# Windowed attention and a top-1 mixture of experts: a smaller ring of keys, and second weights of expert 0 split at the end of attention

## The chip, the cores and the metric

One core of a Trainium2 chip runs the whole program as one launch. The metric is the time of the launch on the device in microseconds (us); lower is better. TensorE is called PE here, VectorE DVE, ScalarE ACT, GpSimd POOL, and SyncE SP; SP issues most of the DMAs and POOL the indirect ones.

## What is computed

Attention over 8 batches, 8 heads, 576 positions and 64 features per head: four heads look back over a window of 32, four over 128 in steps of 4. Its output, 4608 rows of 512, goes into a top-1 mixture of 8 experts with 1024 hidden units.

```python
scores = q @ k.T / sqrt(64), masked by the window of the head
x = softmax(scores) @ v, rows of all heads side by side      # [4608, 512]
logits = x @ w_gate
e = argmax(logits); gate = softmax(logits)[e]
out = gate * (relu(x @ w1[e]) @ w2[e])                        # row by row
```

All of it is in float32. The products of the experts are made from a high and a low part of each operand (`wu` holds both parts of a weight unit, `raw` the unit as loaded): ACT casts `raw` into the high part, and DVE subtracts it from `raw` for the low part.

## The kernel before

**Attention.** 36 tiles of 128 query rows (4 pairs of batches, 9 tiles each) run through a software pipeline, `step(n)`: scores of tile n, transposes of the probabilities of n-1 (`st_trans`, `st_ptcopy`), the product with v and the normalised rows of n-2 (`st_av`, `st_x`), transposes of n-3 and logits of n-4. SP loads q and k of a tile as one transfer (`load_qk`, 576 KB, 128 rows of 4608 bytes) and v as another (`load_v`, 520 KB). The tile `qkr` has 6 slots and `vr` 6; `step(n)` issues `load_qk(n + 5)` and `load_v(n + 3)`. Each tile's keys are loaded whole, that is 128 of its own and the 32 before them.

**Routing.** After the ninth tile of a pair, `route(m)` finds each row's expert and place: logits transposed (`tl`), maximum (`mx`), one-hot (`oh`), running counts (`cs`), and three small matmuls on PE (`rk`, in `rank`), from which DVE selects (`sel`) and works out block and place. For pairs 0 to 2, POOL scatters the row numbers into tables in memory (`tab`). Pair 3 does it on PE instead: for each of its nine tiles DVE makes two matrices, `s` (L554) and `b` (L562) in `mark`, and PE adds their product into `tb` (L573, `enter`). `read_table` reads the three tables back over SP, `add_tables` adds them on POOL (L674, L675), and three DVE instructions make `rows_all` (L437) of `tb` and the tables. From `rows_all` POOL gathers the rows of each expert's blocks (`xg`, L746). While `hold` is on, work set aside for PE waits; it is set for pair 2.

**Experts.** For rows that were routed early, expert 0's first layer (`layer1`: matmuls `s` and `hps`, L900, then `x` and `h` on DVE, L912) runs at the end of attention; its second layer is `layer2` (`yps`, L931). Its second weights are units 4 to 7 of 512 KB; units 4 to 6 are loaded early into `raw`, unit 7 after attention. The rest of the rows of expert 0 comes in blocks `r0`, `r1` (`rest0`): gather, transposes `tpx` (L970), two layers; then experts 1 to 7. From `with tc.manual_schedule` after attention (L1437) the order of all engines is the order of the code.

**What sets the order.** Through step 34 (`MEND`) the order of PE, DVE and ACT is that of the code; behind it, up to L1437, a scheduler orders each engine's instructions by priority. SP's and POOL's order is the scheduler's in all of attention. Each engine executes strictly in the order given. Tiles come from pools; a pool that lies over memory of closed pools first waits for the work on it.

```python
    for key, bufs in (("h", 9), ("w1", 4), ("w2", 4), ("x1", 1), ("d", 1), ("y", 2)):
        pools[key] = ctx.enter_context(tc.tile_pool(name="p" + key, bufs=bufs))
...
    for f in range(4, 8):
        st_.layer1([f])
        raw = early.pop(f) if f in early else st_.load(f)
        st_.units.append(split_unit(1, raw))
```

## Time and profile before

| what | value |
|---|---|
| median of 3 runs | 606.92 us (606.56 to 608.8) |
| the profiled execution, its own time | 606.45 us |
| its span in the trace | 604.7 us |
| PE busy | 585.5 us (97% of the span) |
| DVE, ACT, POOL busy | 363.6, 315.3, 188.3 us |
| mean granted clock of TensorE | 0.991 |
| moved by DMA | 152.52 MB, mean 252 GB/s |

The span is the traced stretch of one execution; the 1.75 us between it and that execution's own time lie around it. In the order of time, attention runs to some 165 us, the routing of the last pair and the first expert's early rows from there to some 195 us, then the experts. A busy time is the sum of an engine's instructions. An idle time counts only where the engine is the one that the end waits for.

### The profile page before, as it was taken

Reading aid. Unit: us, or ns where it says so; the run is one execution under the profiler, and the core shown is the slowest. Engines: PE = TensorE matmul, PEld = TensorE weight load, DVE = VectorE, ACT = ScalarE, POOL = GpSimd, SP = SyncE. Lnnn points to the kernel's source line nnn. Section 1 sums busy time; section 2 is a strip of 40 time slices with the busy share of each in tenths; the row PEclk is TensorE's granted clock in tenths of the full one; section 3 lists DMA queues with packets and bytes.
Section 4 is the critical chain, followed back from the end, with each engine's and each line's share of the span. In section 5 each row is a group of like instructions: output and inputs, shape, how many; then the busy total and the mean of one; then the engine's idle time right before and its main releaser. Section 6 shows DMA issues by size and latency. Waiting matters only on the chain. (4 is left out here: it accounts for less than half of the span.)

```text
span 604.7 us, 13500 instructions
## 1 busy us (share of the span) xinstructions
PE 585.5 (97%) x5175; PEld 478.7 (79%) x5175; DVE 363.6 (60%) x786; ACT 315.3 (52%) x612; POOL 188.3 (31%) x234
## 2 busy tenths in 40 slices
PE   7999999999989999999999999999999999999995
PEld 6877778777777888888888888888888888888784
DVE  3877888887758457636564566457547646663200
ACT  2568776766723555534555466456536554662210
POOL 0346676486573225140033022202300330031011
PEclk8999999999999999999999999999999999999998
DMA  8999999995325538985778679778868786779411
GB/s 333 409 372 412 411 406 408 398 344 162 86 56 176 186 130 278 244 272 171 206 256 298 176 250 296 239 201 288 265 223 241 253 306 173 236 260 405 177 42 46
DMA packets 67522, 152.52 MB, mean 252 GB/s; under 512 B 15040, under 2 KB 31360, under 8 KB 67424
## 3 DMA queue, kind: packets, MB, share of 16 engines
q1 hardware_dynamic: 55744, 121.50, 59.5%
q0 software_dynamic: 11712, 30.14, 14.1%
q8 instruction: 41, 0.67, 0.5%
q14 instruction: 25, 0.20, 0.1%
HBM read 124.02 MB, written 28.60 MB: 252 GB/s over the span
## 5 line engine op out<-in xcount | busy, mean ns | idle before, releaser
L931 PE MATMUL yps<-wu,h 128*128 128x512 f32 x696 | 164.4, 392 | 0.0
L721 DVE TENSOR_TENSOR wu<-raw,wu 128x512 fp32r<-128x512 f32 x200 | 128.3, 687 | 55.7 <-ACT wu L720 49.9
L900 PE MATMUL hps<-x,wu 128*128 128x512 f32 (+1 forms) x720 | 161.6, 383 | 0.2 <-DVE h L912 0.2
L900 PEld LDWEIGHTS hps<-x,wu 128*128 128x128 f32 x720 | 132.3, 188 | 27.4 <-DVE h L912 0.8
L931 PEld LDWEIGHTS yps<-wu,h 128*128 128x128 f32 x696 | 129.4, 188 | 27.4 <-issue 0.6
L720 ACT CAST wu<-raw 128x512 fp32r<-128x512 f32 x200 | 112.9, 618 | 12.2 <-DMA raw<-in_w_dram 11.9
L796 POOL DMA_INDIRECT out_dram<-y,rows_all x30 | 30.4, 1012 | 197.8 <-ACT y L795 85.2
L912 DVE SCALAR_TENSOR_TENSOR h<-hps,h 128x512 fp32r<-128x512 f32 (+1 forms) x60 | 40.2, 671 | 52.4 <-ACT h L911 51.1
L911 ACT ACTIVATE h<-hps 128x512 fp32r<-128x512 f32 (+1 forms) x60 | 35.0, 583 | 62.5 <-PE hps L900 49.6
L323 ACT COPY pts<-pt 96x512 f32<-96x512 f32 x72 | 41.9, 582 | 46.9 <-PE pt L318 40.3
L746 POOL DMA_INDIRECT xg<-x_d,rows_all x30 | 32.0, 1065 | 95.0 <-DVE x L791 35.3
L297 DVE TENSOR_REDUCE nm<-s 128x4 f32<-128x384 f32 x72 | 39.7, 552 | 25.7 <-PE s L286 20.7
L318 PE MATMUL pt<-ident,p 128*96 128x128 f32 x288 | 47.5, 289 | 4.9 <-ACT pts L323 4.2
L795 ACT ACTIVATE y<-yps,gate 128x512 f32<-128x512 f32 x30 | 20.7, 688 | 45.5 <-PE yps L931 37.1
L333 PEld LDWEIGHTS o<-vr,pts 96*64 96x64 f32 x1152 | 37.9, 139 | 7.2 <-issue 6.1
L333 PE MATMUL o<-vr,pts 96*64 96x65 f32 x1152 | 43.1, 226 | 0.4 <-issue 0.4
L302 DVE TENSOR_TENSOR d<-s,nm 128x384 f32<-128x384 f32 x72 | 40.1, 557 | 4.6
L312 ACT ACTIVATE p<-d 128x384 f32<-128x384 f32 x72 | 37.6, 524 | 6.5 <-DVE d L302 6.5
L1037 PE MATMUL ypd<-wu,hd 128*128 128x512 f32 x168 | 40.7, 391 | 0.0
L365 POOL DMA_DIRECT2D x_d<-xs x36 | 20.6, 571 | 63.0 <-DVE xs L353 25.7
L1005 PE MATMUL hpd<-wu,xd 128*128 128x512 f32 x168 | 39.9, 391 | 0.0
L318 PEld LDWEIGHTS pt<-ident,p 128*96 128x96 f32 x288 | 28.9, 128 | 13.0 <-ACT pts L323 5.3
(161 smaller groups left out, 627.0 us busy)
## 6 DMA issues: line engine op xcount, KB each, us to landing
raw<-in_w_dram SPq DMA_DIRECT2D x104, 512.0 KB
qkr<-in_qk_dram SPq DMA_DIRECT2D x36, 576.0 KB
vr<-in_v_dram SPq DMA_DIRECT2D x36, 520.0 KB
rows<-xg SPq DMA_DIRECT2D x29, 264.0 KB
xg<-rows SPq DMA_DIRECT2D x116, 64.0 KB
wu<-in_w_dram SPq DMA_DIRECT2D x12, 512.0 KB
x_d<-xs POOLq DMA_DIRECT2D x44, 128.0 KB
wz<-in_w_dram SPq DMA_DIRECT2D x4, 512.0 KB
```

Source lines behind the costliest of these rows:

```text
L297: nc.vector.tensor_reduce(st["nm", n][:, g], st["s", n][g], axis=AX.X, op=ALU.max)
L302: nc.vector.tensor_tensor(st["d", n][:, g], st["s", n][g], st["nm", n][:, g].broadcast_to([P, HP, KB]), op=ALU.subtract,)
L318: nc.tensor.transpose(pt[:KB, h], st["p", n][:, g, h], ident)
L323: nc.scalar.copy(st["pts", n][:, g], st.pop(("pt", n))[:KB])
L333: nc.tensor.matmul(st["o", n][QB * j : QB * (j + 1), g, h], lhsT=pts[:, g, h, QB * j : QB * (j + 1)], rhs=vr[:KB, n % NRV, a : a + DH + 1] ...
L720: nc.scalar.copy(u[:, 0, sl], raw[:, sl])
L721: nc.vector.tensor_tensor(u[:, 1, sl], raw[:, sl], u[:, 0, sl].bitcast(F32), op=ALU.subtract)
L900: nc.tensor.matmul(hps[:, : self.ns], lhsT=u[:, wpart, fs], rhs=self.x[:, xpart, c, : self.ns], start=(k == 0), stop=(k == 11),)
L912: nc.vector.scalar_tensor_tensor(h[:, 1, :n], hps[:, :n], 0.0, h[:, 0, :n].bitcast(F32), op0=ALU.max, op1=ALU.subtract,)
L931: nc.tensor.matmul(yps, lhsT=self.h[f][:, hpart, ts], rhs=u[:, wpart, fs], start=f == 0 and k == 0, stop=f == 7 and k == 2,)
L1005: nc.tensor.matmul(hps, lhsT=self.x[:, xpart, c], rhs=u[:, wpart, ns], start=(k == 0), stop=(k == 11),)
L1037: nc.tensor.matmul(self.yps, lhsT=self.h[f // 4][:, hpart, f % 4], rhs=u[:, wpart, fs], start=f == 0 and k == 0, stop=f == 7 and k == 2,)
```

## The change

- `qkr` holds q in 5 slots and the keys in a ring of quarters (32 keys each): slot s has quarters 4s+1 to 4s+4, and the 32 keys ahead of a tile are the last quarter of the tile before. A load is one transfer of 128 x 2 x 512 numbers (512 KB); every fifth tile, slot 0, takes two (256 and 320 KB), as its first quarter is loaded too. `vr` has 4 slots. `step(n)` issues `load_qk(n + 3)` and `load_v(n + 1)`. The constants and the host's layout follow.
- Both lie in a pool `ring` of their own that is closed at step 37, and the pool of expert 0's second weights is opened there (`second_pool`). `second_split` splits units 4, 5 at step 38 and unit 6 at step 39; unit 7 is loaded and split behind `layer1(4..7)`.
- The pools after attention have `reuse_waits="tile"`: a tile waits for the tiles that it lies over, not for the pool.
- `mark` takes `rows_f` in a three-operand instruction in place of `pay`; `add_tables` for the whole table goes from POOL, and `rows_out` adds the three tables in five DVE instructions.
- `hold(False)` comes at step 35; `rank` of pair 3, `rows_out` and `layer1(4..7)` get high priority; `layer2` of expert 0 takes units 0 to 3 of both halves ahead of units 4 and 5. The loads of the gate's weights move to step 1.

```diff
...
@@ -196,9 +199,11 @@
     late = att.enter_context(tc.tile_pool(name="late", bufs=1))
     t_in = [late.tile([P, NBK], I32, name=f"t_in{i}") for i in range(3)]
 
-    NRQ, NRV = 6, 6
-    qkr = fix.tile([P, NRQ, QK], F32, name="qkr")
-    vr = fix.tile([P, NRV, VC], F32, name="vr")
+    NRK, NRV = 5, 4
+    ring = ExitStack()
+    ringp = ring.enter_context(tc.tile_pool(name="ring", bufs=1, side="right"))
+    qkr = ringp.tile([P, 2 * NRK * KO + KQ], F32, name="qkr")
+    vr = ringp.tile([P, NRV, VC], F32, name="vr")
     rows_i = fix.tile([P, NPR - 1, NT], I32, name="rows_i")
     rows_f = fix.tile([P, NT], F32, name="rows_f")
     wgz = fix.tile([P, 4, 32], F32, name="wgz")
@@ -206,9 +211,21 @@
     mk = fix.tile([P, QB + NT * NB * KB], BF16, name="mk")
     total = NPR * NT
 
+    q_all = qkr[:, : NRK * KO].rearrange("p (n x) -> p n x", n=NRK)
+    k_all = qkr[:, NRK * KO :].rearrange("p (n h w) -> p n h w", h=HP, w=W)
+
     def load_qk(n):
-        if n < total:
-            nc.sync.dma_start(qkr[:, n % NRQ], qk[n])
+        if n >= total:
+            return
+        slot = n % NRK
+        if slot:
+            here = qkr[:, slot * KO : slot * KO + KO]
+            part = list(here.ap[0])
+            to = bass.AP(here.tensor, here.offset, [part, [NRK * KO + KQ, 2], [1, KO]])
+            nc.sync.dma_start(to, qk[n].rearrange("p (i x) -> p i x", i=2, x=KO + KQ)[:, :, KQ:])
+        else:
+            nc.sync.dma_start(q_all[:, 0], qk[n][:, KQ : KQ + KO])
+            nc.sync.dma_start(qkr[:, NRK * KO : NRK * KO + KQ + KO], qk[n][:, KQ + KO :])
 
     def load_v(n):
         if n < total:
@@ -226,15 +243,14 @@
     nc.sync.dma_start(ident, cst[:, C_ID : C_ID + P])
     load_v(0)
     load_qk(2)
-    load_v(1)
     nc.sync.dma_start(mk[:, mk_a:], mask[:, mk_a:])
-    load_qk(3)
-    load_v(2)
-    nc.sync.dma_start(wgz[:, :, :NE], wg)
-    load_qk(4)
-    nc.sync.dma_start(ca, cst[:, C_TRI:C_ATT])
+
+    def load_gate():
+        nc.sync.dma_start(wgz[:, :, :NE], wg)
+        nc.sync.dma_start(ca, cst[:, C_TRI:C_ATT])
 
     def load_rest():
+        nc.vector.tensor_copy(crun, ca[:, C_C0 - C_TRI : C_C0 + NE - C_TRI])
         nc.sync.dma_start(cc, cst[:, C_ATT:])
         nc.sync.dma_start(rows_i, tok)
         nc.sync.dma_start(rows_f, end)
...
@@ -277,16 +291,16 @@
         st["s", n] = s
 
     def st_scores(n):
-        s, slot = st["s", n], n % NRQ
+        s, slot = st["s", n], n % NRK
         for h in range(HP):
             for j in range(NB):
                 for g in range(2):
                     rows = slice(DH * g, DH * (g + 1))
-                    qo, ko = h * P + QB * j, KO + h * KW + QB * j
+                    qo, ko = h * P + QB * j, 4 * slot + 2 * j
                     nc.tensor.matmul(
                         s[g][QB * j : QB * (j + 1), h],
-                        lhsT=qkr[rows, slot, qo : qo + QB],
-                        rhs=qkr[rows, slot, ko : ko + KB],
+                        lhsT=q_all[rows, slot, qo : qo + QB],
+                        rhs=k_all[rows, ko : ko + 3, h],
                         start=False,
                         stop=h == HP - 1,
                     )
...
@@ -551,11 +565,11 @@
         def mark(t):
             s1 = sp.tile([P, P], F32R, name="s1", bufs=6)
             b1 = sp.tile([P, NBK], F32R, name="b1", bufs=6)
-            v.tensor_scalar(
+            v.scalar_tensor_tensor(
                 s1,
                 ca[:, C_IO - C_TRI : C_IO + P - C_TRI],
                 plc[:, t : t + 1],
-                pay[:, t : t + 1],
+                rows_f[:, t : t + 1].broadcast_to([P, P]),
                 op0=ALU.is_equal,
                 op1=ALU.mult,
             )
@@ -613,7 +627,15 @@
         )
         if m == NPR - 2:
             off_pe(hold, True)
-        on_pe(rank, late=True)
+        if m < NPR - 1:
+            on_pe(rank, late=True)
+        else:
+
+            def rank_first():
+                with tc.high_priority():
+                    rank()
+
+            on_pe(rank_first, late=True)
         off_both(
             select,
             lambda: v.tensor_reduce(
...
@@ -652,13 +673,23 @@
                     off_pe(mark, t)
                 if lo:
                     on_pe(enter, range(lo - 3, lo), late=True)
-            off_pe(
-                lambda: v.tensor_scalar(
-                    scr, box["tb"], 0.0, float(LAST), op0=ALU.is_gt, op1=ALU.mult
-                )
-            )
-            off_pe(lambda: v.tensor_tensor(scr, box["tb"], scr, op=ALU.add))
-            off_pe(v.tensor_tensor, row_i, t_in[0], scr, op=ALU.add)
+
+            def rows_out():
+                with tc.high_priority():
+                    v.tensor_scalar(
+                        scr,
+                        box["tb"],
+                        0.0,
+                        cc[:, C_LP - C_ATT : C_LP + 1 - C_ATT],
+                        op0=ALU.is_gt,
+                        op1=ALU.mult,
+                    )
+                    v.tensor_tensor(scr, box["tb"], scr, op=ALU.add)
+                    v.tensor_tensor(scr, t_in[0], scr, op=ALU.add)
+                    v.tensor_tensor(scr, t_in[1], scr, op=ALU.add)
+                    v.tensor_tensor(row_i, t_in[2], scr, op=ALU.add)
+
+            off_pe(rows_out)
         if after:
             after()
 
@@ -1122,7 +1153,7 @@
     rest0 = [Dynamic(fixed=i, units=statics[0].units) for i in range(EB, 4)]
     first = statics[0]
 
-    todo = {4: [load_rest], 26: [clear_rows]}
+    todo = {1: [load_gate], 4: [load_rest], 26: [clear_rows]}
 
     def at(n, f, *a):
         todo.setdefault(n, []).append(lambda: f(*a))
@@ -1131,7 +1162,6 @@
 
     def read_all():
         read_table(NBK)
-        add_tables(t_in[0], NBK)
 
     def early_fetch():
         def fetch():
@@ -1166,6 +1196,19 @@
     for u in range(4, 7):
         at(total + u - 4, early_load, u)
 
+    def second_pool():
+        ring.close()
+        pools["w", 1] = pools["w1"] = ctx.enter_context(
+            tc.tile_pool(name="pw1", bufs=4, side="right", reuse_waits="tile")
+        )
+
+    def second_split(u):
+        first.units.append(split_unit(1, early.pop(u)))
+
+    at(total + 1, second_pool)
+    for u in range(4, 7):
+        at(total + 2 + (u - 4) // 2, second_split, u)
+
     def early_layer1(f):
         n = first.ns
         hps = psa.tile([P, 512], F32, tag=f"S{f % 2}", name="s")
@@ -1187,8 +1230,8 @@
         if not turning or taken[0]:
             pull_pe(late=True)
         go(st_scores, n)
-        load_qk(n + 5)
-        load_v(n + 3)
+        load_qk(n + 3)
+        load_v(n + 1)
         turned = turning.pop(0) if turning and not taken[0] else None
         if turned is not None:
             first.turn_x(turned)
@@ -1222,6 +1265,8 @@
         pull_off()
         go(st_logits, n - 4)
         go(st_keep, n - 4)
+        if n == total - 1:
+            hold(False)
         pull_pe(late=True)
         go(st_mask, n + 1)
         if spare:
@@ -1250,10 +1295,14 @@
     att.close()
 
 
-    pools["ps"] = ctx.enter_context(tc.tile_pool(name="ps", bufs=2, space=PSUM))
-    for key, bufs in (("h", 9), ("w1", 4), ("w2", 4), ("x1", 1), ("d", 1), ("y", 2)):
-        pools[key] = ctx.enter_context(tc.tile_pool(name="p" + key, bufs=bufs))
-    pools["w", 1], pools["w", 2], pools["x", 1] = pools["w1"], pools["w2"], pools["x1"]
+    pools["ps"] = ctx.enter_context(
+        tc.tile_pool(name="ps", bufs=2, space=PSUM, reuse_waits="tile")
+    )
+    for key, bufs in (("h", 9), ("w2", 4), ("x1", 1), ("d", 1), ("y", 2)):
+        pools[key] = ctx.enter_context(
+            tc.tile_pool(name="p" + key, bufs=bufs, reuse_waits="tile")
+        )
+    pools["w", 2], pools["x", 1] = pools["w2"], pools["x1"]
 
     NJ = 2 * NE
 
@@ -1429,10 +1478,9 @@
 
     st_, nx = statics[0], statics[1]
     a, c = 0, 2
-    for f in range(4, 8):
-        st_.layer1([f])
-        raw = early.pop(f) if f in early else st_.load(f)
-        st_.units.append(split_unit(1, raw))
+    with tc.high_priority():
+        st_.layer1(range(4, 8))
+    st_.units.append(split_unit(1, st_.load(7)))
     r0, r1 = rest0
     with tc.manual_schedule(engines=ENGS | {mybir.EngineType.Pool, mybir.EngineType.SP}):
         ahead = nx.ahead
@@ -1460,9 +1508,11 @@
         nx.fetch(1)
         for u in range(3):
             bring(u)
-        st_.layer2(0, range(6))
+        st_.layer2(0, range(4))
+        st_.layer2(1, range(4))
         some(3)
-        st_.layer2(1, range(6))
+        st_.layer2(0, range(4, 6))
+        st_.layer2(1, range(4, 6))
         some(5)
         r0.prep_x()
         nx.fetch(2)
```

In the built programs DVE's queue around the last pair's logits, behind the last attention tile's rows (`xs`): `lt`, `mx` and `sh` are the routing, `x` the low part of the first layer's output. Before:

```order
L353 TENSOR_TENSOR xs<-o,rz 128x512
L536 SCALAR_TENSOR_TENSOR at_i<-blk_i,wide 128x1
L912 SCALAR_TENSOR_TENSOR x<-s,x 128x256 x2
L496 TENSOR_REDUCE lt<-tl 128x24
L912 SCALAR_TENSOR_TENSOR x<-s,x 128x256
L496 TENSOR_REDUCE lt<-tl 128x24 x2
L581 TENSOR_REDUCE mx<-lt 128x9
L582 TENSOR_TENSOR sh<-lt,mx 128x72
L585 SCALAR_TENSOR_TENSOR cand<-sh,ca 128x72
L586 TENSOR_REDUCE fst<-cand 128x9
L603 TENSOR_REDUCE se<-ex 128x9
L589 TENSOR_TENSOR oh<-cand,fst 128x9x8
```

With the change:

```order
L367 TENSOR_TENSOR xs<-o,rz 128x512
L752 TENSOR_TENSOR wu<-raw,wu 128x512 x3
L943 SCALAR_TENSOR_TENSOR x<-s,x 128x256
L752 TENSOR_TENSOR wu<-raw,wu 128x512 x2
L943 SCALAR_TENSOR_TENSOR x<-s,x 128x256
L752 TENSOR_TENSOR wu<-raw,wu 128x512
L510 TENSOR_REDUCE lt<-tl 128x24
L752 TENSOR_TENSOR wu<-raw,wu 128x512
L943 SCALAR_TENSOR_TENSOR x<-s,x 128x256
L510 TENSOR_REDUCE lt<-tl 128x24 x2
L752 TENSOR_TENSOR wu<-raw,wu 128x512
L595 TENSOR_REDUCE mx<-lt 128x9
```

Eight subtractions `wu` of units 4 to 7, which stood behind the marks, now stand between `xs` and `mx`. Farther on the last `x`, which stood behind `cs`, stands between `sh` and `cand`; `many` and `crun`, which stood behind `sel`, stand ahead of it; and one `b` instead of two stands ahead of the first `s`.

PE's queue from the three `rk` of pair 3 to the first products `tb` of its marks. Before:

```order
L900 MATMUL s<-x,wu 128x256 x11
L522 MATMUL rk<-crun,cc 128x72
L525 MATMUL rk<-oh,ca 128x72
L526 MATMUL rk<-cs,cc 128x72
L900 MATMUL hps<-x,wu 128x256 x18
L573 MATMUL tb<-b_3507,s_3506 128x320
L900 MATMUL hps<-x,wu 128x256
L573 MATMUL tb<-b_3511,s_3510 128x320
```

With the change:

```order
L536 MATMUL rk<-crun,cc 128x72
L931 MATMUL s<-x,wu 128x256 x2
L931 MATMUL hps<-x,wu 128x256 x6
L539 MATMUL rk<-oh,ca 128x72
L931 MATMUL hps<-x,wu 128x256
L540 MATMUL rk<-cs,cc 128x72
L931 MATMUL hps<-x,wu 128x256 x29
L587 MATMUL tb<-b_3530,s_3529 128x320
L587 MATMUL tb<-b_3534,s_3533 128x320
L587 MATMUL tb<-b_3538,s_3537 128x320
L587 MATMUL tb<-b_3542,s_3541 128x320
```

The matmuls `hps` and `s` of the first layer that stood among the marks now stand ahead of the first `tb`: 36 `hps` instead of 18.

DVE's queue from the last mark to `rows_all`. Before:

```order
L562 TENSOR_SCALAR b_3543<-cc,blk 128x320
L912 SCALAR_TENSOR_TENSOR h<-hps,h 128x256
L656 TENSOR_SCALAR scr<-tb 128x320
L721 TENSOR_TENSOR wu<-raw,wu 128x512
L660 TENSOR_TENSOR scr<-tb,scr 128x320
L721 TENSOR_TENSOR wu<-raw,wu 128x512
L437 TENSOR_TENSOR rows_all<-t_in_108,scr 128x320
```

With the change:

```order
L576 TENSOR_SCALAR b_3566<-cc,blk 128x320
L943 SCALAR_TENSOR_TENSOR h<-hps,h 128x256
L679 TENSOR_SCALAR scr<-tb,cc 128x320
L943 SCALAR_TENSOR_TENSOR h<-hps,h 128x256
L687 TENSOR_TENSOR scr<-tb,scr 128x320
L943 SCALAR_TENSOR_TENSOR h<-hps,h 128x256
L688 TENSOR_TENSOR scr<-t_in_108,scr 128x320
L943 SCALAR_TENSOR_TENSOR h<-hps,h 128x256
L689 TENSOR_TENSOR scr<-t_in_109,scr 128x320
L690 TENSOR_TENSOR rows_all<-t_in_110,scr 128x320
```

Two more additions stand ahead of `rows_all`, and the subtractions `wu` are gone from there.

## Rows read from the trace of the kernel before

**Rows 1.** PE's waits, whole run: us in total, times, longest us.

```profile
PE pt L318 <- ACT pts L323: 4.2, 6, 1.1
PE tb L573 <- DVE s L554: 2.1, 1, 2.1
```

**Rows 2.** Busy time by stretch; its first row names the columns.

```profile
core 0: us, PE busy (x) PEld busy (x) DVE busy (x) ACT busy (x) POOL busy (x), PEclk, DMA share, GB/s
60.00:80.00 20.00, 18.51 (x380) 15.54 (x381) 17.51 (x50) 14.99 (x31) 13.87 (x19) 1.00 1.03 413
...
150.00:160.00 10.00, 8.55 (x152) 6.85 (x142) 8.10 (x21) 7.80 (x18) 4.68 (x8) 1.00 0.37 106
170.00:180.00 10.00, 7.60 (x60) 7.00 (x59) 6.79 (x32) 2.24 (x6) 7.30 (x8) 1.00 0.20 60
180.00:190.00 10.00, 8.87 (x50) 6.85 (x49) 9.79 (x24) 4.36 (x10) 4.23 (x4) 1.00 0.31 78
200.00:540.00 340.00, 340.00 (x1536) 281.19 (x1535) 202.11 (x342) 181.49 (x331) 71.67 (x68) 1.00 0.75 235
```

**Rows 3.** SP's queue, 5 to 150 us: what its issues waited for.

```profile
SPq L211 <- PE s L286: 20.4, 11, 3.1
...
SPq L211 <- DMA qkr<-in_qk_dram: 8.8, 8, 1.5
```

**Rows 4.** Tile qkr: count, min/median/max ns, first and last start.

```profile
L286 PE MATMUL s<-qkr x1152: 240/243/364, 5.6 to 155.3; 64*64 64x96 f32 x192
```

**Rows 5.** DVE by time: start us, us, instruction, [idle before].

```profile
165.53 0.69 DVE L353 TENSOR_TENSOR xs<-o,rz 128x512 f32<-128x512 f32 x1
...
172.00 0.56 DVE L496 TENSOR_REDUCE lt<-tl 128x24 f32<-128x96 f32 x2
172.60 0.23 DVE L581 TENSOR_REDUCE mx<-lt 128x9 f32<-128x72 f32 x1
...
173.99 0.31 DVE L592 TENSOR_TENSOR_SCAN cs<-ca,oh 128x72 f32<-128x72 f32 x1
174.22 0.40 DVE L912 SCALAR_TENSOR_TENSOR x<-s,x 128x256 fp32r<-128x256 f32 x1
...
176.32 0.23 DVE L530 TENSOR_TENSOR sel<-rk,oh 128x72 f32<-128x72 f32 x1 [1.58 <-PE rk L526]
176.47 0.29 DVE L608 COPY many<-gate 128x144 f32<-128x144 f32 x1
...
177.62 0.57 DVE L562 TENSOR_SCALAR b<-cc,blk 128x320 fp32r<-128x320 f32 x1
178.18 0.37 DVE L562 TENSOR_SCALAR b<-cc,blk 128x320 fp32r<-128x320 f32 x1
178.48 1.01 DVE L554 TENSOR_SCALAR s<-ca,plc,pay 128x128 fp32r<-128x128 f32 x3
...
180.81 0.90 DVE L554 TENSOR_SCALAR s<-ca,plc,pay 128x128 fp32r<-128x128 f32 x1
...
186.76 0.48 DVE L437 TENSOR_TENSOR rows_all<-t_in,scr 128x320 int32<-128x320 int32 x1
```

**Rows 6.** Groups of instructions, 160 to 200 us: busy us, mean ns of one.

```profile
L721 DVE TENSOR_TENSOR wu<-raw,wu 128x512 fp32r<-128x512 f32 x8 | 5.2, 685 | 1.0 <-DMA raw<-in_w_dram 1.0
```

**Rows 7.** PE in order of time, 172 to 197 us.

```profile
174.67 2.42 PE L900 MATMUL hps<-x,wu 128*128 128x256 f32 x18
179.22 0.42 PE L573 MATMUL tb<-b,s 128*128 128x320 f32 x1 [2.13 <-DVE s L554]
...
195.37 0.60 PE L970 MATMUL tpx<-ident,xg 128*128 128x128 f32 x4
```

**Rows 8.** POOL in order of time, 172 to 190 us.

```profile
180.59 1.03 POOL L674 TENSOR_TENSOR t_in<-t_in,t_in 128x320 int32<-128x320 int32 x1 [1.46 <-DMA t_in<-tab]
...
187.53 1.54 POOL L746 DMA_INDIRECT xg<-x_d,rows_all  x1 [4.24 <-DVE rows_all L437]
```

**Rows 9.** DMA queues between 187.5 and 193.3 us: packets, MB, share.

```profile
q0 software_dynamic: 79, 0.28, 24.6%
```

More of the change, by code (lines that the diff above doesn't have):

```diff
@@ L254, in attention_moe_kernel @@
         nc.tensor.matmul(warm_ps, lhsT=cold, rhs=cold, start=True, stop=True)
-    nc.vector.tensor_copy(crun, ca[:, C_C0 - C_TRI : C_C0 + NE - C_TRI])
     st = {}
@@ L511, in route @@
         ]
-        wide, pay = [small(n, (P, NT)) for n in ("wide", "pay")]
+        wide = small("wide", (P, NT))
         load = small("load", (P, NT), I32)
@@ L646, in route @@
                 lambda: v.tensor_copy(plc, plc_i),
-                lambda: v.tensor_tensor(pay, rows_f, plc, op=ALU.subtract),
             )
```

15 lines of the change are left out of this document (9 added, 6 removed).

## The prediction

> **What bounds the kernel now.** I read the busy times by stretch first. They should show where PE, the engine that ends the run, is not working: from 200 to 540 us PE is busy for 340.00 of 340.00 us, so an edit there can only change work that PE hides, while 150 to 160, 170 to 180 and 180 to 190 us leave 1.45, 2.40 and 1.13 us idle, 4.98 us in all [rows 2]. Next come PE's waits, for their causes. The longest single one is 2.1 us, the first product `tb` waiting for DVE's `s`; the transposes of attention wait 4.2 us in six pieces for ACT [rows 1]. No wait for a transfer is among them. Third comes SP's queue: key loads wait 20.4 us for PE's scores, so most of them start when a slot comes free, and 8.8 us for landings of earlier transfers [rows 3]. Last come DVE, PE and POOL by time in the transition, where the chain is: logits, `mx`, `cs`, `sel`, marks, `tb`, `rows_all`, POOL's gather, and then PE's `tpx` at 195.37 us, behind which PE never waits up to 540 us [rows 2, 5, 7, 8]. So the whole change is worth what it moves that `tpx`, plus what it does to PE in attention.
>
> **Keys, values and the lookahead: 0 us.** A load now goes out when the scores four steps ahead of its own have read the slot. The scores run from 5.6 to 155.3 us in 36 tiles [rows 4], so a step is about 149.7/35 = 4.28 us, and four are 17.1 us; less about 1 us for the scores themselves, 16 us are left. In the stretch from 60 to 80 us the DMA engines are full at 413 GB/s [rows 2]. At most the keys and values of three tiles stand ahead, 3 x 1.1 MB, and a weight unit of 0.5 MB: 3.9 MB, or 9.4 us at that rate. So about 6 us are spare. The values have the same four steps between their readers. Bytes fall: 28 loads of 576 KB become 512 KB, 1.8 MB in all, 4 us of DMA time that PE does not see. The eight additional DMAs, SP's six loads of constants that now stand ahead of tile 8 instead of 10, and the three weight loads that stand farther ahead in SP's queue now, each waiting for a split on POOL, all fall within those 6 us. A later first mask could cost up to 0.3 us; I take 0 and keep 0.3 for the range. `wgz` and `ca` are first needed four steps in: 0.
>
> **DVE ahead of the routing: later.** Eight subtractions of 0.685 us [rows 6], 5.5 us, move ahead of `mx`. From the end of `xs`, 166.22, to `mx` at 172.60 [rows 5] DVE has three `x` (0.40 each) and three `lt` (two in 0.56), 2.0 us of work, and about 4.3 us of waiting that the subtractions can fill. What does not fit is 5.5 - 4.3 = 1.2 us; one more short wait for an `x` of ACT makes it 1.6, so `mx` at 174.2. If all of it lay beside waits it would be 0, if none, 5.5. Between `mx` and `cs` one `x` of 0.40 and the small gate step of 0.2 come in, so `cs` ends 2.2 us later than at 174.30, at 176.5. Then `sel`: before, it came 2.0 us behind the end of `cs` and was idle for 1.58 us of it, released by the last `rk` [rows 5]; PE's queue has one `hps` between `rk` and `rk` now. Between nearly no lag and that one I take the middle, a `sel` 1.2 us behind, at 177.7.
>
> **The marks: shorter.** From `sel` to the first `tb` it was 179.22 - 176.32 = 2.9 us [rows 5, 7]. `many` and `crun` go ahead of `sel` (0.3 us, by the row of `many`), `pay` goes (about 0.1), and one `b` (0.37) less stands ahead of the first `s`: 2.1 us are left, so the first `tb` at 179.8; with 0.5 for the waits between engines, 180.3, that is 1.1 us late. Of the later marks, an `s` took 0.90 us at 180.81, where a usual one takes a third of 1.01. It began while POOL's addition of the tables ran, 180.59 to 181.62, and ended with it [rows 5, 8]; a second one did the same. Without the additions on POOL these two give back 2 x 0.56 = 1.1 us. The Trainium skill, SBUF — State Buffer, section Who interferes with whom, says that a DVE instruction with two SBUF inputs waits for a GpSimd instruction that reads SBUF. By that rule the three-operand `s` would be held as the old one was; what gives the 1.1 us back is POOL's silence, and by the rule alone, with POOL at work, the sum would be 1.1 us worse. So the last `tb` ends about where it did, near 184.9 us instead of 184.7.
>
> **`rows_all`: later.** Before it was ready at 187.24 [rows 5]. Two more additions of 0.48 us stand in the chain, and the two subtractions of 0.685 are gone from it; the four `h` between them take part of that place. From 184.9, five additions at some 0.42 a piece and two `h` of 0.42 give 187.9 (187.4 to 188.6).
>
> **Gather and PE.** POOL's gather started 0.29 us behind `rows_all`, at 187.53 [rows 8]. By 193.3 POOL's queue had moved 0.28 MB, one block of 128 rows of 2112 bytes being 0.27 MB [rows 9], so it had landed 5.7 us after its start. Taken again: 187.9 + 0.3 + 5.7 = 193.9. PE itself would be there sooner. From the first `tb` to `tpx` it took 16.15 us [rows 7]. Now 18 `hps` stand ahead of the first `tb` instead of among the marks; 18 of them took 2.42 us [rows 7]. The waits of 1.13 us between 180 and 190 [rows 2] go too: 16.15 - 2.4 - 1.1 = 12.6, so PE is ready at 180.3 + 12.6 = 192.9 and waits 1 us for the gather. `tpx` starts at 193.9 instead of 195.37: **1.4 us gained**. The rule that speaks otherwise is in the Trainium skill, DMA: Bandwidth & Descriptors, section Anatomy of one DMA — SWDGE (gpsimd) path: a DMA from POOL takes about 2.0 us and its bytes by 436 GB/s. By that the gather would be estimated at 2.6 us, would land near 191, and PE alone would set `tpx`, 2.5 us earlier than before; the row shows more than twice that time, with weight loads beside it, so the row stands in my sum.
>
> **The rest: 0 us.** Pools that wait by tile take away waits of ACT and DVE behind the marks; PE's part of it is within the 1.13 us counted. Behind `tpx` PE has as many instructions as before, and from 200 to 540 us it waits for nothing [rows 2]; the new order of `layer2` moves matmuls without changing their number. The early `hold(False)` and the earlier scatters of pair 2 bring the tables in sooner: needed only at `rows_all`.
>
> **The sum.** Its own time of the profiled execution is 606.45 us; less 1.4 and with 0.2 for the first mask, 605.2 or so. The median of the runs before stands 0.5 above that execution, and by that it would be 605.7; I forecast 605.5. From no change a measurement of this kernel can tell about 0.5%, 3.0 us.
>
> **The rivals.**
> *First, the gather does not bind.* By the reckoning above PE is ready at 192.9; with `sel` following at once (1.0 us) and ACT's waits in attention gone too (1.45 us between 150 and 160 us [rows 2]), up to 4.98 us go: 601.5 to 603.9. For it: the routing no longer has PE waiting 2.13 us at the first `tb` [rows 7], as 36 `hps` cover it. Against it: `rows_all` comes later in every version of the sum, and PE cannot pass the `tpx` that needs it.
> *Second, the routing eats it all.* DVE is the bound of the transition already (9.79 of 10 us between 180 and 190 [rows 2]). If none of the subtractions finds a wait (up to 5.5 us instead of 1.2), or unit 7 lands late while DVE stands before its subtraction, `rows_all` comes at 189.5 to 191 and `tpx` at 195.5 to 197: 606.5 to 608.
> *Third, slower: the keys come late.* While the DMA engines are full, in the stretch around 60 to 80 us, they may be so full that the shorter lookahead shows. It decides when more than 16 us x 413 GB/s = 6.6 MB stand ahead of a load, or SP stands that long at a weight load for a split on POOL. Each tile then waits in PE: five tiles by 1 us give 610, ten by 1 us 615. For it: share 1.03 of the DMA engines [rows 2], and three weight loads moved into that stretch. Against it: PE has no wait for a transfer today, and my count finds 3.9 MB.
> *Fourth, nothing moves.* PE could be held in the transition by as much as before, by another wait; 606.5.
>
> **How the numbers follow.** The forecast has a chance of 0.45, the first rival 0.24 (four fifths of it beyond 0.5%), the second 0.14, the third 0.09, the fourth 0.08. Faster by over 0.5%, under 603.9: 0.20. Slower by over 0.5%, above 609.9: 0.09, the third rival. The rest, 0.71, is within 0.5%. The range reaches from most of the first rival, 602.4, to the second, 608.0.
>
> **What would show it.** In the profile of the changed kernel `mx` at about 174, `cs` ending near 176.5, the first `tb` near 180.3, no `s` of 0.9 us, `rows_all` near 187.9, `tpx` near 193.9 with PE waiting about 1 us for the gather, and scores that never wait for a load. A PE idle time that names a transfer of `qkr` or `vr` proves the third rival; a `tpx` with no wait ahead of it near 192.9 or less, the first; `rows_all` behind 189, the second. I should be wrong most easily in the 4.3 us of waiting that I fill with subtractions, and in the 5.7 us of the gather.

## The result, and the profile after

The changed kernel takes 612.61 us in the median of 7 runs (610.89 to 614.47), the kernel before 607.77 us in 7 runs beside them (606.56 to 609.21). The ratio is 1.0076, with a 95% interval of 1.0056 to 1.0096: slower, by some 4.6 us. Forecast were 605.5 us and, most likely, no change that can be told. A second timing gave 1.0087 (1.0062 to 1.0112).

The profiled execution has 612.61 us as its own time and a span of 610.8 us, 6.1 above that of before. PE is busy for 590.7 us instead of 585.5 with the same number of matmuls, POOL for 185.0 instead of 188.3. Busy time by stretch, columns as in [rows 2]:

```profile
60.00:80.00 20.00, 18.56 (x389) 15.35 (x383) 17.12 (x48) 15.93 (x34) 13.67 (x20) 1.00 1.03 402
...
180.00:190.00 10.00, 9.77 (x64) 8.50 (x63) 9.45 (x33) 1.32 (x4) 1.69 (x2) 1.00 0.24 58
190.00:200.00 10.00, 8.07 (x36) 6.31 (x35) 3.79 (x10) 0.68 (x2) 4.82 (x5) 0.92 0.80 272
200.00:540.00 340.00, 339.96 (x1522) 279.18 (x1521) 198.24 (x336) 179.01 (x326) 69.38 (x67) 1.00 0.77 232
```

PE is idle for 1.93 us between 190 and 200 us, and the granted clock there is 0.92 in the mean, so for a part of the stretch the lower of its two levels. But from 200 to 540 us PE is as busy as before [rows 2] and runs 1522 matmuls in that time instead of 1536: in the mean they are slower, and the experiments show which. PE's waits, the ones of [rows 1] and the new ones:

```profile
PE pt L332 <- ACT pts L337: 2.9, 5, 0.8
...
PE tpx L1001 <- DMA xg<-x_d,rows_all: 1.9, 1, 1.9
...
PE tp L399 <- ACT wu L751: 1.0, 1, 1.0
PE rk L539 <- DVE oh L603: 1.0, 1, 1.0
```

The wait for `s` ahead of `tb` is gone, one for the gather has come, one stands ahead of `tp`, the transposes of the last attention tile, and none names `qkr` or `vr`. DVE in the transition, as in [rows 5]; `z` is the step ahead of `xs`:

```profile
168.03 0.17 DVE L357 TENSOR_SCALAR z<-o 128x8 f32<-128x8 f32 x1 [3.37 <-PE tp L399]
...
168.47 0.69 DVE L367 TENSOR_TENSOR xs<-o,rz 128x512 f32<-128x512 f32 x1
...
171.79 1.29 DVE L752 TENSOR_TENSOR wu<-raw,wu 128x512 fp32r<-128x512 f32 x2 [0.44 <-ACT wu L751]
...
177.06 0.22 DVE L595 TENSOR_REDUCE mx<-lt 128x9 f32<-128x72 f32 x1
...
178.97 0.31 DVE L606 TENSOR_TENSOR_SCAN cs<-ca,oh 128x72 f32<-128x72 f32 x1
...
179.81 0.23 DVE L544 TENSOR_TENSOR sel<-rk,oh 128x72 f32<-128x72 f32 x1 [0.26 <-PE rk L540]
...
182.56 0.34 DVE L568 SCALAR_TENSOR_TENSOR s<-ca,plc,rows_f 128x128 fp32r<-128x128 f32 x1
...
187.12 0.55 DVE L679 TENSOR_SCALAR scr<-tb,cc 128x320 f32<-128x320 f32 x1
187.59 0.41 DVE L943 SCALAR_TENSOR_TENSOR h<-hps,h 128x256 fp32r<-128x256 f32 x1
187.91 0.48 DVE L687 TENSOR_TENSOR scr<-tb,scr 128x320 f32<-128x320 f32 x1
188.31 0.41 DVE L943 SCALAR_TENSOR_TENSOR h<-hps,h 128x256 fp32r<-128x256 f32 x1
...
189.42 0.42 DVE L943 SCALAR_TENSOR_TENSOR h<-hps,h 128x256 fp32r<-128x256 f32 x1 [0.30 <-ACT h L942]
...
190.28 0.49 DVE L690 TENSOR_TENSOR rows_all<-t_in,scr 128x320 int32<-128x320 int32 x1
```

PE there, as in [rows 7], and POOL's gather and ACT's first `h`:

```profile
183.13 1.67 PE L587 MATMUL tb<-b,s 128*128 128x320 f32 x5
...
186.77 0.31 PE L587 MATMUL tb<-b,s 128*128 128x320 f32 x1
...
192.45 3.01 PE L962 MATMUL yps<-wu,h 128*128 128x512 f32 x12
197.39 0.63 PE L1001 MATMUL tpx<-ident,xg 128*128 128x128 f32 x4 [1.93 <-DMA xg<-x_d,rows_all]
...
199.90 3.84 PE L1036 MATMUL hpd<-wu,xd 128*128 128x512 f32 x12
```

```profile
191.04 1.00 POOL L777 DMA_INDIRECT xg<-x_d,rows_all  x1 [9.36 <-DVE rows_all L690]
```

```profile
186.29 0.94 ACT L942 ACTIVATE h<-hps 128x256 fp32r<-128x256 f32 x3 [8.39 <-DVE s L568]
```

The gather lands 6.35 us after its start (197.39 - 191.04), and the 12 `hpd` behind PE's wait take 3.84 us. In a second profile of the same kernel, with nearly the same wait but a granted clock of 1.00 from 190 to 200 us, they take 2.90:

```profile
194.86 0.63 PE L1001 MATMUL tpx<-ident,xg 128*128 128x128 f32 x4 [1.84 <-DMA xg<-x_d,rows_all]
...
196.72 2.90 PE L1036 MATMUL hpd<-wu,xd 128*128 128x512 f32 x12
```

Where the time went, by stages of PE, from the starts of its matmuls: A, from the start of the span to the first scores of the last attention tile; B, from there to the 13th `hpd` (the second dozen of `r0`); C, to the last `hpd`; D, to the end of the span (us).

```
kernel                     A       B       C      D     span
before                   154.50  45.80  316.54  87.84  604.67
before, second profile   155.69  45.94  317.79  87.89  607.31
after                    156.00  47.93  318.75  88.10  610.78
after, second profile    153.55  46.26  319.27  88.61  607.69
after, third profile     154.56  46.11  318.65  89.38  608.70
```

A varies by 2 us and more between executions of one kernel, so the 1.5 us that it is longer in the first profile prove nothing. C is longer by 2.1 to 2.7 us in all three than in the first profile of before (in its second, one wait of 1.2 us for an `h` lies in C), and no step of the prediction had touched it. The second and third profile of the changed kernel are of executions of 609.52 and 610.53 us, faster than its medians; what its slower executions lose, no profile shows.

### The profile page after: what moved, and what is told of

It reads as the page before. It is cut to its first block, busy times and chain, and to the rows that moved or that the text cites. A ratio compares the mean times of both kernels' runs of the same rounds, so it can differ in the third digit from the quotient of the medians.

```text
span 610.8 us, 13506 instructions
## 1 busy us (share of the span) xinstructions
PE 590.7 (97%) x5175; PEld 480.9 (79%) x5175; DVE 363.5 (60%) x787; ACT 315.3 (52%) x612; POOL 185.0 (30%) x232
## 4 chain that ended last, share of the span: by engine, by line
PE 66%; issue 2%; DMA 2%; POOL 0%; ACT 0%; POOLq 0%
PE hps L931 25%; PE yps L962 25%; PE hpd L1036 6%; PE ypd L1068 6%; DMA xg<-x_d,rows_all 1%; PE tph L1053 1%; PE ypt L1136 1%; PE hpt L1115 1%; DMA out_dram<-y,rows_all 0%; PE tpx L877 0%; DMA x_d<-many 0%; PE tpx L1001 0%; POOL out_dram L827 0%; ACT y L826 0%; POOLq L1693 0%
```

## The experiments

All ratios are to runs of the kernel before on the same chip, beside the kernel's own; the chips differ by up to 1%. The intervals are of 95%.

**Both kernels once more, for the scatter of one profile.** No edit.

> The kernel before, unaltered, for a second profile. Start theory: the scores of tile 4 begin near 22.0 us again. Spread theory: they begin anywhere from 22 to 23.5, or the stretch from 200 to 540 us shows stalls of 0.1 us that add up to 1 to 2 us. In both the first tpx of r0 has no wait ahead of it.

> The changed kernel, unaltered, for a second profile. Gather theory: PE again waits 1.5 to 2.5 us at the first tpx of r0 behind the gather, and its clock is at 1.2 GHz for some 3 us behind it. Start theory: the scores of tile 4 again begin near 23.4 us, 1.4 later than before the change, since the clock rises later with the new order of loads. Spread theory: the start or the stretch from 200 to 540 us comes out differently by 1 to 2 us, as it differs between executions of one kernel.

One execution each: 609.09 us and 609.52 us, beside a median before of 607.67 (604.37 to 609.31, 23 runs). The stages are in the table above. A start of attention that is 1.4 us late in one profile of the changed kernel is not late in the next, so what looked like a later start is scatter.

**The ring alone.** The kernel before with the ring, its layout, the loads three tiles ahead and the gate's loads at step 1, and nothing else:

```diff
-    NRQ, NRV = 6, 6
-    qkr = fix.tile([P, NRQ, QK], F32, name="qkr")
+    NRK, NRV = 5, 4
+    qkr = fix.tile([P, 2 * NRK * KO + KQ], F32, name="qkr")
...
-        load_qk(n + 5)
-        load_v(n + 3)
+        load_qk(n + 3)
+        load_v(n + 1)
```

> The kernel before with the new layout of keys, the ring of 5 and 4 slots, the loads three tiles ahead and the gate's weights at step 1, and nothing else. Gather theory: the loss is all at the end of attention, so this is within 0.5 us of before. Start theory: 1.4 to 1.7 us slower than before, ratio 1.002 to 1.003. If late keys cost more than that, PE waits that name transfers, and a ratio over 1.004.

608.36 us (605.74 to 612.72, 12 runs), ratio 1.0025 (1.0002 to 1.0048). A little slower, and no wait of PE names a key. The ring by itself is not the 0.8%.

**The gather's wait filled.** Six `yps` of expert 0 ahead of `tpx`:

```diff
         some(5)
+        st_.layer2(1, range(6, 8))
         r0.prep_x()
...
-        st_.layer2(1, range(6, 8))
         r0.layer2(range(4))
```

> The changed kernel with the last six matmuls of the second half's layer2 moved from behind r0's turn to ahead of the first tpx of r0, so that PE has 2.3 us more to do there. Gather theory: the wait of 1.93 us and the slow clock behind it go, 2 to 3.5 us less than the changed kernel, unless the six are missed where they stood; 609 to 610.5. Start and spread theories alone: no more than 1 us less than the changed kernel.

PE's wait at `tpx` fell to 0.4 us; 610.49 us (12 runs), ratio 1.0048 (1.0029 to 1.0068). The wait is a part of the loss at most: the intervals of this kernel and of the changed one overlap, and C is still 318.65 us.

**Where the second weights lie.** The built programs show what the diff does not: the new pool of expert 0's second weights, which later holds, among others, the first weights of experts 2 and 5, begins at byte 196576 of a partition; before, it began at 131744. Modulo 256 that is 224 instead of 160, and 160 is where every other pool of weights, `x` and `h` begins, in both kernels. A 64-byte tile ahead of the ring moves it to 196512, 160 again:

```diff
     NRK, NRV = 5, 4
+    pad = ctx.enter_context(tc.tile_pool(name="pad", bufs=1, side="right"))
+    pad.tile([P, 16], F32, name="pad")
     ring = ExitStack()
```

> The changed kernel with 64 bytes of padding at the top of memory, so that expert 0's second weights, and every third expert's, start at byte 196512 of a partition instead of 196576; the order of instructions is the same. Alignment theory: the matmuls that read these weights lose the 7 ns each, the stretch from the 13th hpd to the last is 316.5 to 317 us again instead of 318.7 to 319.3, and the run is 2 to 3 us shorter than the changed kernel. Height theory (weights that lie high in memory are read slower): no change. Gather theory of the transition: no change, 1.5 to 2 us of waiting at the first tpx stay.

> The changed kernel again, timed on the chip of the next three. 1.005 to 1.009 of before. The slow matmuls of every third expert and the wait at tpx are there again; the spread between executions is wider than that of before.

> The changed kernel with the 64 bytes of padding again, beside the changed kernel on one chip. Alignment theory: 2.5 to 3 us less than the changed kernel, ratio to before 1.002 to 1.005. If the ring is the larger part (code loading and the spread of attention): less than 1.5 us of difference between the two.

On one chip the changed kernel took 613.12 us, ratio 1.0087 (1.0062 to 1.0112), and this one 610.58, ratio 1.0043 (1.0017 to 1.0068), 12 runs each, intervals that just overlap; on another chip it gave 1.0069 (1.0039 to 1.0099), 7 runs. C is 316.66 and 317.35 us, as before the change. The rows of `hps`, grouped by form, show it best; the last number is the mean ns of one. Expert 1, whose first weights lie elsewhere, and expert 2, whose first weights are in that pool, in the changed kernel:

```profile
L931 PE MATMUL hps<-x,wu 128*128 128x512 f32 x96 | 22.0, 390 | 0.0
...
L931 PE MATMUL hps<-x,wu 128*128 128x512 f32 x96 | 22.6, 395 | 0.0
```

Expert 2 with the 64 bytes:

```profile
L933 PE MATMUL hps<-x,wu 128*128 128x512 f32 x96 | 21.9, 389 | 0.0
```

The matmuls overlap, so the mean hides the size of it: between the starts of two `hps` lie 226.7 ns, and 233.4 in the slow ones (the starts of 96 in a row, averaged), 3%. It holds for the `hps` of experts 2 and 5 and in part for `yps`, `hpd` and `ypd` that read the pool.

**The same put into the kernel before.** 64 bytes ahead of each of two pools of weights, and nothing else:

```diff
+        if key in ("w1", "w2"):
+            gap = ctx.enter_context(tc.tile_pool(name="gap" + key, bufs=1))
+            gap.tile([P, 16], F32, name="gap")
         pools[key] = ctx.enter_context(tc.tile_pool(name="p" + key, bufs=bufs))
```

> The kernel before with a gap of 64 bytes ahead of the pool of expert 0's second weights (131744 becomes 131808, 32 becomes 96 after division by 128) and one behind it, so that all other pools lie as before; PE's order is unchanged. Alignment theory: the matmuls of every third expert take some 7 ns more (first layer) and 3 ns more (second layer), the stretch from the 13th hpd to the last is 2 us longer than before (318.5 to 319.3), ratio 1.003 to 1.006. If the slow matmuls came from the high place or from what lies beside it there: no change.

606.24 us beside 602.18 on its chip, ratio 1.0064 (1.0041 to 1.0088): the kernel before becomes slower by some 4 us from 128 bytes of memory that nothing uses. C is 320.52 us, 4.0 longer. Its profile tells more than the expectation asked, for the second gap doesn't put the pools behind it back but moves them by 64 bytes more. The pools begin at 224 (`w1`) and 32 (`w2` and the second `x`) modulo 256; the other pools of weights and `x`, opened earlier, and `h` stay at 160. The `hps` of experts 1, 2, 3 and 5:

```profile
L900 PE MATMUL hps<-x,wu 128*128 128x512 f32 x96 | 21.9, 390 | 0.0
...
L900 PE MATMUL hps<-x,wu 128*128 128x512 f32 x96 | 22.6, 396 | 0.0
...
L900 PE MATMUL hps<-x,wu 128*128 128x512 f32 x96 | 22.5, 395 | 0.0
...
L900 PE MATMUL hps<-x,wu 128*128 128x512 f32 x96 | 22.1, 392 | 0.0
```

Set beside the starts of the two operands, weights (stationary) and `x` (moving), modulo 256 bytes; every operand's offset within its tile is a multiple of 256, so these are also where the operands begin. The addresses are those of the built programs; no profile lists them. Two numbers in the last column are the two halves of the 96, where they differ:

```
kernel                expert  weights   x   mean ns   interval over 226.6 ns
after                   1       160   160    390        1.1, 0.1
after                   2       224   160    395        6.7
64 bytes ahead          2       160   160    389        0.1
before with gaps        1        32    32    390        0.5, 0.2
before with gaps        2       224   160    396        6.7
before with gaps        3       160    32    395        5.9
before with gaps        4        32   160    395        6.8, 6.7
before with gaps        5       224    32    392        2.4, 2.3
before with gaps        6       160   160    390        1.0, 0.2
```

Expert 1 runs at full speed with both operands at 32, expert 3 doesn't with weights at 160, where they were fast before. So it is not the place of the weights that counts, but that the two operands of a matmul begin at the same place modulo 256.

**Other distances.** The same padding with 32 and with 96 bytes, weights at 192 and 128 modulo 256:

```diff
-    pad.tile([P, 16], F32, name="pad")
+    pad.tile([P, 8], F32, name="pad")
```

> The changed kernel with 32 bytes of padding: the second weights start at a remainder of 64. Same reading as the last: tells which of the four remainders of 32 bytes are slow. No change of the transition.

> The changed kernel with 96 bytes of padding: the second weights start at a multiple of 128. Alignment theory, if it is the remainder of 128 and its distance from that of the other operands (32): the 7 ns are gone or smaller; if only the remainder 32 is good, they stay. No change of the transition.

One execution each, 609.45 and 606.72 us, beside 602.18. In both the `hps` of expert 2 have a mean of 395 ns, 6.7 ns over in the interval, and C is 319.05 and 319.37 us. Of the four distances tried in this pool only that of 160 to 160 is free.

**The pool left in its old place.** The ring closed, but the second weights' pool opened after attention, as before, and units 4 to 7 split behind `layer1`:

```diff
-    for u in range(4, 7):
-        at(total + 2 + (u - 4) // 2, second_split, u)
...
-    for key, bufs in (("h", 9), ("w2", 4), ("x1", 1), ("d", 1), ("y", 2)):
+    for key, bufs in (("h", 9), ("w1", 4), ("w2", 4), ("x1", 1), ("d", 1), ("y", 2)):
```

> The changed kernel with the pool of expert 0's second weights where it was before, between h and the next weights (131744 to 164512 of a partition), and all pools of the experts at their old addresses; the eight subtractions of units 4 to 7 then stand behind rows_all. Alignment and height theories both: the stretch from the 13th hpd to the last is 316.5 to 317 us. Gather theory: mx and rows_all come 2 to 3 us earlier after the scores of tile 35, and the wait at tpx for the gather goes; but PE waits for the weights ahead of layer2 instead, up to 3 us. Sum 2 to 4 us less than the changed kernel; if neither theory holds, no change.

The profiled execution had no slow `hps` and no wait at `tpx`, but two of 1.0 us for the late split, and a span of 603.5 us. The timed runs went from 604.50 to 612.33 us: 609.02 in the median of 6, ratio 1.0108 (1.0074 to 1.0142), so its profile is of one of its two fastest executions. C is 317.20 us, near what both theories of the address asked, but the 2 to 4 us less that were expected did not come. What its slower executions wait for no profile shows; the run does not settle anything.

**The transition, in two steps.** First the nine `h` tiles moved from memory where the marks' `s` and `b` lie, for which ACT waited 8.39 us; then also units 6 and 7 split behind `rows_all` (`True` pins their subtractions there):

```diff
-    for key, bufs in (("h", 9), ("w2", 4), ("x1", 1), ("d", 1), ("y", 2)):
+    for key, bufs in (("w2", 4), ("x1", 1), ("h", 9), ("d", 1), ("y", 2)):
```

```diff
-    for u in range(4, 7):
-        at(total + 2 + (u - 4) // 2, second_split, u)
+    for u in range(4, 6):
+        at(total + 2, second_split, u)
...
-    st_.units.append(split_unit(1, st_.load(7)))
+    st_.units.append(split_unit(1, early.pop(6), True))
+    st_.units.append(split_unit(1, st_.load(7), True))
```

> The changed kernel with the pools of the next weights and x1 opened ahead of h, so that h no longer lies over the marks' s and b; the additions of rows_out then stand together and the four h behind rows_all. Gather theory: rows_all 1.2 to 1.6 us earlier, the wait at tpx 0.3 us instead of 1.9, 1.5 to 2 us less in all. If the gather does not bind: no change, or later by what PE waits for h. The slow matmuls of every third expert stay.

> As the last one, and the four subtractions of units 6 and 7 pinned behind rows_all. Gather theory: mx 1.5 to 2.7 us earlier after the scores of tile 35, rows_all 2.5 to 4 us earlier than the changed kernel, no wait at tpx for the gather; then PE itself sets it, 2 to 3 us less than the changed kernel. Against it: PE may wait for units 6 and 7 in layer2. The slow matmuls of every third expert stay.

PE's wait at `tpx` was 1.1 us with the first, forecast 0.3, and none with both; B went to 43.51 and 42.81 us, against 45.33 in the kernel with 64 bytes of padding on this chip. The 45.80 of before can't stand beside them, as it was taken on another chip: the kernel before with its gaps, on a third, has 44.07. Both still have the misplaced pool (C 320.36 and 318.36 us). Timed, 1.0083 (1.0064 to 1.0102) and 1.0079 (1.0057 to 1.0101), 6 runs each, no better than the changed kernel elsewhere and the padded one here (606.85 us); 1.5 to 3 us less than the changed kernel were expected. By these short timings the gain of the profiles is not shown; the next runs show it.

**Old slots and a mended version.** The kernel with 64 bytes of padding, with the six old slots, the old layout and the loads five and three tiles ahead; and the same with the two steps above:

```diff
-    NRK, NRV = 5, 4
+    NRQ, NRV = 6, 6
...
-        load_qk(n + 3)
-        load_v(n + 1)
+        load_qk(n + 5)
+        load_v(n + 3)
```

> The changed kernel with the padding and with the ring undone: old layout of keys, six slots each, loads five and three tiles ahead, gate's weights loaded at the start; all the rest of the change stays. Ring theory (PE stands still in attention where its code comes late, more often with the smaller ring): 1 to 2 us less than the padded kernel, PE's waits that are put down to issue back to 0.2 to 0.6 us up to 165 us, and a spread like that of before. Otherwise as the padded kernel. To before: within 1 us.

> The ring undone, the padding, h not over the marks' tiles, and units 6 and 7 split behind rows_all. If the three causes (alignment, ring, gather) are all there is: 2.5 to 3.5 us less than before, ratio 0.994 to 0.996, with the scores of tile 35 to the 13th hpd in 42.8 us instead of 45.8, the stretch from there to the last hpd in 316.5 to 317.4, and no wait at tpx. If something else is lost: the same as before.

On the chip where the changed kernel took 613.12 us and the padded one 610.58, the old slots gave 608.66, ratio 1.0026 (0.9994 to 1.0057), and the mended transition 605.58, ratio 0.9963 (0.9941 to 0.9985), 12 runs each: faster than both kernels. The waits put down to `issue` up to 165 us did not fall with the old slots as expected, to 0.2 to 0.6 us: they are 1.9 us there, 2.3 in the padded kernel and 0.7 in the mended one. The step from 608.66 to 605.58 has intervals that don't overlap. Its PE and DVE in the transition:

```profile
188.46 1.59 PE L924 MATMUL hps<-x,wu 128*128 128x256 f32 x12
...
194.21 0.60 PE L994 MATMUL tpx<-ident,xg 128*128 128x128 f32 x4
194.56 1.63 PE L955 MATMUL yps<-wu,h 128*128 128x512 f32 x6
196.03 2.97 PE L1029 MATMUL hpd<-wu,xd 128*128 128x512 f32 x12
```

```profile
184.76 0.55 DVE L670 TENSOR_SCALAR scr<-tb,cc 128x320 f32<-128x320 f32 x1 [0.56 <-PE tb L578]
185.34 0.49 DVE L678 TENSOR_TENSOR scr<-tb,scr 128x320 f32<-128x320 f32 x1
...
186.98 0.49 DVE L681 TENSOR_TENSOR rows_all<-t_in,scr 128x320 int32<-128x320 int32 x1
187.39 1.09 DVE L936 SCALAR_TENSOR_TENSOR h<-hps,h 128x256 fp32r<-128x256 f32 x3
```

No `h` stands among the additions any more, from the last `tb` (184.41 + 0.31) to the end of `rows_all` it is 2.75 us instead of 3.69, `tpx` does not wait, and the `hpd` behind it run at full speed.

**The ring in the mended version.** The same with the ring and the short lookahead back, on two chips, the second time beside the version with the old slots:

> The fastest version so far (padding, h apart, units 6 and 7 late) with the small ring and its late loads put back. Ring theory: 1 to 2 us slower than that version, that is 0.998 to 1.001 of before, with more of PE's waits put down to issue up to 165 us and a wider spread. If the ring costs nothing: 0.994 to 0.998 of before.

> Theory (the ring of quarters with the shorter lookahead costs 0.2 to 0.45%, also where nothing else of the change is left): this kernel, with the old 6 slots of qkr and vr and loads five and three tiles ahead, comes at 0.995 to 0.998 of the kernel before on this chip, and 1 to 2.5 us under the kernel with the ring beside it. Rival (the difference between the two earlier timings was one of chips): both come within 1 us of each other, each at 0.997 to 1.001.

> Theory (the ring costs): 0.999 to 1.002 of the kernel before, 1 to 2.5 us above the kernel with the old six slots on the same chip; its profile shows no wait of PE for qkr or vr all the same. Rival (chips differ): 0.997 to 1.001 and within 1 us of the other.

First 603.21 us, ratio 1.0008 (0.9987 to 1.0030); then 608.04 us, 1.0002 (0.9974 to 1.0030), with the old slots beside it at 606.02, 0.9980 (0.9958 to 1.0002), 12 runs each. In the medians the ring is slower in each of three pairs: by 0.7 us (before, and the ring alone), 1.9 us (old slots, and padding alone) and here 2.0 us; in the last two the intervals overlap. The old-slot version's runs go from 603.76 to 609.79, the ring's from 602.67 to 611.12. In the two profiles, PE between 40 and 60 us, with old slots and with the ring:

```profile
40.00:60.00 20.00, 18.76 (x403) 14.66 (x403) 14.43 (x34) 15.96 (x35) 10.83 (x16) 1.00 1.02 408
```

```profile
40.00:60.00 20.00, 17.85 (x377) 13.86 (x375) 13.74 (x32) 14.57 (x32) 10.37 (x16) 1.00 1.04 409
```

and the wait of the ring's kernel that the other lacks, in the matmuls `o` with the values, put down to no tile:

```profile
PE o L349 <- issue: 2.1, 4, 1.0
```

By the last attention tile all but 0.43 us of it is made good (A 154.20 and 154.63 us). Of the 1.59 us between the two spans the largest part, 0.90, arises in D (88.22 and 89.12), where a second layer, `ypd`, waits for ACT's `hd`; over the whole run, with old slots and with the ring:

```profile
PE ypd L1061 <- ACT hd L1050: 0.3, 1, 0.3
```

```profile
PE ypd L1072 <- ACT hd L1061: 1.0, 2, 0.7
```

Ahead of `hd` in ACT's queue stand casts of a weight unit, and for that unit ACT had waited, again with old slots and with the ring:

```profile
517.82 1.14 ACT L742 CAST wu<-raw 128x512 fp32r<-128x512 f32 x2 [1.26 <-DMA raw<-in_w_dram]
```

```profile
519.42 1.14 ACT L753 CAST wu<-raw 128x512 fp32r<-128x512 f32 x2 [2.18 <-DMA raw<-in_w_dram]
```

In 9 of the 14 profiles of kernels with the ring `ypd` is idle there for 0.3 to 1.0 us; in the 6 with old slots it is 0.1 at most. So the ring most likely costs 0.1 to 0.3%, but by what path is open: no wait names a key or value, `issue` is only what is left when no releaser is found, and why a weight unit should come later at the end of the run was not tried.

## Why the prediction was wrong

**The bound and the rows were read rightly; the step that failed is "The rest: 0 us".** It took from "PE is busy for 340.00 of 340.00 us" [rows 2] that nothing in the experts can change unless instructions are added. Busy time says how long the matmuls take, not that they take as long as before. The change moves a pool of weights to the other side of the memory, which the prediction described only as a pool, and never priced. It costs 2.2 us in stage C (316.54 to 318.75), of which 1.3 are the 192 `hps` of experts 2 and 5 at 6.7 ns, gives back 2.5 us when 64 bytes are put in (613.12 to 610.58), and, put into the kernel before, costs some 4 us by itself, there with more pairs of operands apart.

**"DVE ahead of the routing" was sized rightly, but from a start that came late.** Counted from the first scores of the last tile, `mx` was forecast 19.7 us behind (174.2 - 154.5) and came at 21.06 (before: 18.10). From the end of `xs` to `mx` it was 7.90 us instead of 6.38, so 1.5 us of the subtractions' 5.5 came through, forecast 1.6. But `xs` itself, ahead of every subtraction, ended 13.16 us behind the scores instead of 11.72: 1.44 us that the term had at nothing, as it took the time of `xs` from the rows of before. DVE's `z` stood still for 3.37 us there, put down to PE's `tp`, though by PE's own records, whose ends are modelled, the `o` that `z` reads ended at 166.43, 1.6 us earlier. The late `xs` (13.15 to 13.30) is in all nine profiles of the changed kernel and its variants on chips where the kernel before takes 607.5 us and more; it is in none of the seven on chips where that takes 602 to 603 (11.61 to 11.65), and not in the kernel with the ring alone (11.63). What holds DVE there is open. `sel` followed 0.53 us behind the end of `cs`, not 1.2: the middle between no lag and the old one was too long.

**"The marks: shorter" held in its sum, with luck in the parts.** From `sel` to the end of the last `tb` it was 7.27 us, forecast 7.2; but the first `tb` came 3.3 us behind `sel` instead of 2.6, and the rest of the marks made it good. No `s` took 0.90 us any more; they take 0.34 with POOL's additions gone.

**"`rows_all`: later" and "Gather and PE" were mis-sized.** From the last `tb` to the end of `rows_all` it was 3.69 us instead of 3.0: three `h` stand between the five additions, not two, one of them with 0.30 us of waiting for ACT, and an addition takes 0.48 to 0.55 us. The gather took 6.35 us instead of 5.7. With these, `tpx` came 41.39 us behind the scores instead of 39.4, the sum of +1.44 for `xs`, -0.08 from there to `mx`, and -0.08, -0.67, +0.07, +0.69 and +0.62 for `cs`, `sel`, the marks, `rows_all` and the gather. PE waited 1.93 us, forecast 1. So the 1.4 us to be gained were a loss of 0.5 us (40.87 before): the transition went the way of the second rival, if not by its mechanism. Its sign, `rows_all` at 189.5 to 191, was seen at 190.77; without the 1.5 us by which this execution's A is longer, which prove nothing, it is 189.27, just short of it. In the execution of the profile the clock then fell to 0.92 in the mean, and from `tpx` to the 13th `hpd` PE took 6.54 us, against 4.95 in the second profile at 1.00: another 1.6 us, in that execution alone.

**"Keys, values and the lookahead: 0 us" was nearly right.** The third rival had the right sign by a wrong mechanism: no wait for a key or value was seen, in any profile. The ring alone measures 0.25% (0.02 to 0.48%); where it sits is open, so that the 0 was a little too good. The later first mask, put at 0 in the term and at 0.2 us in the sum, was a wait of 0.4 to 0.6 us in four of the 14 profiles with the ring, and of 0.4 in one of the six with old slots.

What of the 5.6 us (613.12 against 607.5 on one chip) each part holds, by the medians of that chip: 2.5 for the weights' place, 1.9 for the ring and lookahead, its intervals overlapping, and 1.2 for the rest, whose interval (0.9994 to 1.0057) holds no change too. Mending the transition then takes 3.1 off. A gain over the kernel before is shown with the old slots alone: 0.9963 on one chip, and 0.9980 on another, where the interval ends at 1.0002. With the ring, the address and the transition both mended, the kernel stands at 1.0008 and 1.0002 of before, so the address alone did not hide the forecast's gain.

## What to carry to other kernels

When a change moves a pool, look up where its tiles begin in memory, beside those that the same matmuls read; a PE that is busy all the time can still be slower, and the mean of one kind of matmul, expert by expert, shows it where waits don't. A chain's instruction that must come early is to be freed on its own queue from what stands between (here `h` and the splits of weights), and a tile put over the memory of the work that it runs beside waits for that work, by tile or not. When one gain fails to show, mend the causes one after the other on one chip.

## What the runs showed of the hardware

- **The matmuls `hps` (128x128 by 512 columns) start every 226.7 to 227.7 ns, where no wait falls among them, when their two operands begin at the same place modulo 256 bytes, and every 232.5 to 233.4 ns when the weights begin 32, 64, 128 or 224 bytes behind `x`; the one pair 192 apart took 229.** The weight loads of these `hps` take 188 or 189 ns in both cases; it is the matmul whose record is longer. The Trainium skill, SBUF — State Buffer, section Who interferes with whom, gives PE two read ports, for the moving operand and for the weight load, independent of each other. It says nothing of their addresses; in these runs they matter, by 3%. What inside does it was not tried, nor were other shapes or types.
- **The clock fell behind a short wait, but not always.** Of eight profiles in which PE waited 1.6 to 2.2 us at `tpx`, three show a granted clock below full from 190 to 200 us (0.92 in the changed kernel, 0.88 with 64 bytes of padding, 0.83 with 32: a part of the time at 1.2 GHz instead of 2.4), five show 1.00. The kernels without the wait, before and the mended one among them, show 1.00 there; the one with the pool left in its old place shows 0.88 from 180 to 190 us, where PE waits twice for 1.0 us. Why it falls in some executions only was not found.
